# Attention with a fused maxout layer: a fifth group transposed by DMA, loads placed behind the crossbar transposes, the last tile stored by halves

## The chip, the cores and the metric

The kernel runs on one core of a Trainium2 chip. The metric is device time in microseconds, from the start of the program to its end. TensorE (PE) does the matmuls, VectorE (DVE) and ScalarE (ACT) work on elements, GpSimd (POOL) copies and issues loads, SyncE (SP) issues transposes and stores. Each engine runs its own list of instructions in order and waits at semaphores for the others. POOL, SP and ACT each have a queue of their own for the DMAs that they issue; the 16 DMA engines of the core are common to all.

## What is computed

Attention over 8 batches, 12 heads, 448 positions and 64 dimensions, with one added to the softmax's denominator, and behind it a layer that takes the larger of three projections:

```python
scores = scale * np.matmul(q, k.transpose(0, 1, 3, 2))
m = np.max(scores, axis=-1, keepdims=True)
e = np.exp(scores - m)
attn = e / (np.sum(e, axis=-1, keepdims=True) + np.exp(-m) + 1e-09)
x = np.matmul(attn, v)          # then (B*S, H*D) = (3584, 768)
h = np.maximum(np.maximum(x @ w1, x @ w2), x @ w3)   # each 768 x 768
out = h @ w_out
```

All inputs and the output are float32 in memory; the loads convert to float16.

## The kernel before

**Groups.** Heads are taken four at a time (GH = 4): 3 groups to a batch, 24 groups in all, numbered i. A batch is complete for the projections when its three groups are.

**What a group needs.** load_qk(i) issues the loads of k and q, load_v(i) those of v in two parts, all from POOL (lines 103, 113, 116). The q and k of a group must be transposed to have the head dimension on the partitions. For the first groups (i < PE_QK) transpose_pe does this in two halves of 11 PE transposes each (line 181), and an engine given as an argument evicts the results from PSUM (evac, lines 168 and 170). For the others transpose_dma issues two crossbar DMA transposes from SP, of q and then of k (line 211), and shift_q afterwards moves blocks of the result between the partition halves with four copies (line 219). prep_v (lines 357 to 360) copies v into the layout that the matmuls read: on DVE for the first groups, on POOL for i >= PE_QK.

**Buffers.** Loaded tiles have four buffers of each kind, KT and QT (the transposed k and q) three, the prepared v three. The transpose of group i+2 can therefore start only when the scores of group i-1 are done. The PSUM pool ps_s has three buffers, shared by score tiles, attention results and PE transposes of the later first groups.

**The order of work.** It is written out by hand. After a prologue, batch 0's three groups are done by halves (parts "E" and "O"), which gives the up-projections something to start on. Then the main loop runs over i = 3 to 23. Each iteration has three visits (vi = 0, 1, 2): scores of group i for two, two and three units (scores, line 274, and their exps on ACT, line 294); in the first two visits the attention of group i-1 (av_tail, line 314, reading vt, then av_main, line 331, and the normalization on DVE); then filler. x_transpose_dma(i-1) puts the attention's result into xT with one crossbar transpose from SP (line 384).

**Filler.** A list of pieces: up_piece (line 401: six or more matmuls, result taken over by DVE at 410 or 412) and out_piece (line 424: a tile of 128 rows by 384 columns; DVE scales it into o_sb at 431). add_batch(b) appends a batch's pieces at the visits given in the dictionary adds, fill(cols) takes as many as the given number of columns pays for, and share(n) spreads what is left evenly up to the next addition. Whatever is left after the loop runs at the end, then all of the last batch.

**Stores.** When both column halves of an output tile are in o_sb, two stores of 64 rows each go out on SP (line 443), one behind the other.

**POOL's list in the main loop** is, for each iteration: the loads of v for group i+2 and of k, q for group i+3; prep_v(i), if i >= 6; shift_q(i+2), which waits for the crossbar transpose. SP's is: two transposes of group i+2, the x transpose of group i-1, and stores as they fall due.

Of the kernel before, what the change touches and what calls it, by code (L numbers as in the profile page):

```python
# [12 lines left out]
AF = mybir.ActivationFunctionType  # L13
ALU = mybir.AluOpType
ts = bass.ts

MMDT = FP16
LAMBDA = 256.0
# [3 lines left out]
def kernel(  # L22
# [29 lines left out]
    scale = 1.0 / math.sqrt(D)  # L52


    PE_QK = 6
    NEB = 2
    NV = 3

# [49 lines left out]
    def load_v(i):  # L108
        b, g = groups[i]
        t = ld_pool.tile([P, GH, 5, D], MMDT, tag="ld_v", name="ld_v")  # L110
        raw.setdefault(i, {})["v"] = t
        src = v[b].rearrange("(g h) (p t) d -> g p h (t d)", g=NG, t=T)[g]
        nc.gpsimd.dma_start(  # L113
            out=t[0:HP, :, 1:5].rearrange("p h t d -> p h (t d)"), in_=src[:, :, 0 : 4 * D]
        )
        nc.gpsimd.dma_start(  # L116
            out=t[HP:P, :, 0:4].rearrange("p h t d -> p h (t d)"), in_=src[:, :, 3 * D : T * D]
        )
# [53 lines left out]
    def transpose_pe(i, pr, pool, k_eng, q_engs):  # L172

        if pool is ps_s:
            both = ps_s.tile([128, 2, 1024], MMDT, tag="s", name="trT")
            tps = [both[:, 0], both[:, 1]]
        else:
            tps = [ps_b.tile([128, 1024], MMDT, tag="b", name="trT") for _ in range(2)]
        kr, qr = raw[i]["k"], raw[i]["q"]
        def tr(n, j, src, t):  # L180
            nc.tensor.transpose(  # L181
                out=tps[n][:, ts(j, 128)],
                in_=src[:, t + 1 : t + 3, :].rearrange("x t d -> x (t d)"),
                identity=ident16,
            )

        kj = (0, 1, 2) if pr == 0 else (3, 4, 5, 6)
        qt = (-1, 1, 3, 5, 0, 2, 4, 6) if pr == 0 else (8, 10, 12, 7, 9, 11, 13)
        for j, b in enumerate(kj):
            tr(0, j, kr, 2 * b)  # L190
        for j, t in enumerate(qt):
            tr(1, j, qr, t)
        if i not in KT:
            KT[i] = att_pool.tile([P, T * 128], MMDT, tag="KT", name="KT")
            QT[i] = att_pool.tile([P, (NB + 1) * 128], MMDT, tag="QT", name="QT")
        evac(
            k_eng,
            KT[i][:, kj[0] * 128 : (kj[-1] + 1) * 128],
            tps[0][:, 0 : len(kj) * 128],
        )  # L200
        q0 = pr * 1024
        n = -(-len(qt) // len(q_engs))
        for e, eng in enumerate(q_engs):
            a, b = e * n * 128, min((e + 1) * n, len(qt)) * 128
            evac(eng, QT[i][:, q0 + a : q0 + b], tps[1][:, a:b])
# [10 lines left out]
    def shift_q(i, eng):  # L216
        t = QT[i]
        for d0, s0, o, a, n in ((0, HP, 1, 4, 3), (HP, 0, 0, 4, 4), (0, HP, 11, 7, 4), (HP, 0, 11, 8, 3)):
            eng.tensor_copy(  # L219
                out=t[d0 : d0 + HP, o * 128 : (o + n) * 128],  # L220
                in_=t[s0 : s0 + HP, a * 128 : (a + n) * 128],
            )
# [131 lines left out]
    def prep_v(i, eng):  # L354
        t = raw[i].pop("v")
        vx, vt = v_buf[i % NV], vt_buf[i % NV]
        eng.tensor_copy(out=vx[:, :, :, 0:D], in_=t[:, :, 1:4, :])  # L357
        t2 = t.rearrange("p (r h) t d -> p r h t d", r=NP)
        eng.tensor_copy(out=vt[0:HP, :, 0:D], in_=t2[0:HP, :, 0, 4, :])
        eng.tensor_copy(out=vt[HP:P, :, 0:D], in_=t2[HP:P, :, 1, 0, :])  # L360
# [53 lines left out]
    NH = 2  # L414
    NW = DM // NH
    order = (0, 2, 4, 6, 1, 3, 5)

    def out_piece(bp, t, nh):
        if nh == 0:
            outs[0] = out_pool.tile([128, DM], FP32, tag="o_sb", name="o_sb")  # L420
        o_sb = outs[0]
        op_ps = ps_b.tile([128, 512], FP32, tag="b", name="op_ps")
        for fc in range(NFC):
            nc.tensor.matmul(  # L424
                out=op_ps[:, 0:NW],
                lhsT=hT[bp][:, fc, ts(t, 128)],
                rhs=wout_sb[:, fc, ts(nh, NW)],
                start=(fc == 0),
                stop=(fc == NFC - 1),
            )  # L430
        nc.vector.tensor_scalar(  # L431
            out=o_sb[:, ts(nh, NW)],
            in0=op_ps[:, 0:NW],
            scalar1=1.0 / LAMBDA,
            scalar2=None,
            op0=ALU.mult,
        )
        if nh == NH - 1:
            for half in range(2):
                n = 2 * t + half  # L440
                b = 2 * bp + n // T
                rows = out[b * S : (b + 1) * S].rearrange("(p t) m -> t p m", t=T)
                nc.sync.dma_start(out=rows[order[n % T]], in_=o_sb[half * HP : half * HP + HP])


    UP = NDC * (S + 6)
# [20 lines left out]
    def fill(cols):  # L467
        credit[0] += cols
        while pieces and credit[0] > 0:
            f, a, w = pieces.pop(0)  # L470
            f(*a)
            credit[0] -= w
        if not pieces:
            credit[0] = min(credit[0], 0.0)
# [24 lines left out]
    for n, (part, g) in enumerate(parts):  # L499
        ej = n % NEB  # L500
        pp, pg = parts[n - 1] if n > 0 else (None, None)
        step = UPE if n > 2 else 0
        nxt = g + 1 if part == "E" and g < NG - 1 else None
        scores(g, ej, (0, 1), part)
        if n != 3:
            scores(g, ej, (2, 3), part)
        if n > 0:
            av(pg, 1 - ej, 0, pp)
        if n > 1 and n != 4:
            x_transpose_pe(parts[n - 2][1], parts[n - 2][0])  # L510
        if n == 3:
            av(pg, 1 - ej, 1, pp)
            scores(g, ej, (2, 3), part)
        fill(step)
        if nxt is not None and n > 0:
            transpose_pe(nxt, 0, ps_b, AC, (DV,))
        fill(step)
        scores(g, ej, (4, 5), part)
        scores(g, ej, (6,), part)
        if n == 0:  # L520
            warm(4)
            transpose_pe(nxt, 0, ps_b, DV, (DV,))
        if n == 3:
            x_transpose_pe(pg, pp)
            add_up(0, 0, NE, [(i, f) for i in range(3) for f in (0, 2, 4)])
        if nxt is not None:
            transpose_pe(nxt, 1, ps_b, DV, (DV,))
        if n > 0 and n != 3:
            av(pg, 1 - ej, 1, pp)
        fill(step)  # L530
        if n == 5:
            transpose_pe(3, 1, ps_s, DV, (DV,))
        fill(step)
        if n == 0:
            prep_v(0, DV)
        if n == 1:
            load_weight(2)
        if n == 2:
            load_v(3)
            load_qk(4)  # L540
            load_weight(3)
        if n == 4:
            load_v(4)
            load_qk(5)
            transpose_pe(3, 0, ps_s, DV, (DV,))


    visits = ((0, 1), (2, 3), (4, 5, 6))
    adds = {3 * (3 * b + 4) + 1: b for b in range(1, B - 1)}

    def share(n):

# [3 lines left out]
    for i in range(3, NI):  # L556
        ej, pj = (i + 1) % NEB, i % NEB
        first = i == 3
        if i + 2 < NI and i + 2 >= PE_QK:
            transpose_dma(i + 2)  # L560
        if first:
            load_v(5)
            load_qk(6)
        elif i + 2 < NI:
            load_v(i + 2)
            if i + 3 < NI:
                load_qk(i + 3)
        for vi, units in enumerate(visits):
            n = 3 * i + vi
            scores(i, ej, units)  # L570
            if vi < 2:
                av(i - 1, pj, vi, "O" if first else "EO")
            if vi == 1:
                prep_v(i, nc.vector if i < PE_QK else nc.gpsimd)
                if not first:
                    x_transpose_dma(i - 1)
            if n in adds:
                add_batch(adds[n])
            per = UPE if first and vi < 2 else share(n)
            if vi == 0 and first:  # L580
                x_transpose_pe(1, "O")
            if vi == 2 and first:
                fill(per / 2)
                x_transpose_pe(i - 1, "O")
                add_up(0, NE, NO, [(w, f) for w in range(3) for f in (0, 2, 4)])
                add_out(0)
                per = share(n)
            if vi > 0 and i + 1 < PE_QK:
                fill(per / 2)
                transpose_pe(i + 1, vi - 1, ps_s, DV, (DV,))  # L590
                fill(per / 2)
            else:
                fill(per)
        if i + 2 < NI and i + 2 >= PE_QK:
            shift_q(i + 2, nc.gpsimd)

    av(NI - 1, NI % NEB, 0, "EO")
    av(NI - 1, NI % NEB, 1, "EO")
# [34 lines left out]
```

The softmax here doesn't subtract the row's maximum and nothing guards it: scores larger than these inputs give would overflow.

## Time and profile before

| | |
|---|---|
| median of 8 runs | 343.94 us (343.52 to 344.77) |
| the profiled execution, its own time | 343.89 us |
| its span in the profile | 342.0 us |
| PE clock granted | 1.0 of full speed |
| HBM read, written | 44.04 MB, 11.01 MB |

The profile is of one execution. Its span runs from the first to the last instruction; the time of the execution is 1.9 us longer. Of what follows, a timeline line has start, length, engine, line, operation, output and inputs, how many instructions are merged in it and, in brackets, how long the engine had been idle and what ended that. A line of the table of waits has who waited for whom, total us, how often, and the longest. The slices on the page are 40 equal parts of the span with the busy share in tenths.

The costliest groups (line, engine, operation, output and inputs, shape, count, busy us and mean ns of one, idle us before it and its releaser):

```profile
L294 ACT ACTIVATE e<-stp 128x896 f16<-128x896 f32 (+4 forms) x171 | 144.0, 903 | 145.0 <-PE stp L274 144.9
L401 PE MATMUL p_i<-xT,w 128*128 128x448 f16 (+2 forms) x972 | 173.6, 332 | 0.5 <-DVE o_sb L431 0.3
```

PE spends half its time in up_piece and hardly ever waits there; ACT idles as long as it works, waiting for scores.

### The profile page before, as it was taken

Reading aid. Unit: us, or ns where it says so; the run is one execution under the profiler, and the core shown is the slowest. Engines: PE = TensorE matmul, PEld = TensorE weight load, DVE = VectorE, ACT = ScalarE, POOL = GpSimd, SP = SyncE. Lnnn points to the kernel's source line nnn. Section 1 sums busy time; section 2 is a strip of 40 time slices with the busy share of each in tenths; the row PEclk is TensorE's granted clock in tenths of the full one; section 3 lists DMA queues with packets and bytes.
Section 4 is the critical chain, followed back from the end, with each engine's and each line's share of the span. In section 5 each row is a group of like instructions: output and inputs, shape, how many; then the busy total and the mean of one; then the engine's idle time right before and its main releaser. Section 6 shows DMA issues by size and latency. Waiting matters only on the chain.

```text
span 342.0 us, 9746 instructions
## 1 busy us (share of the span) xinstructions
PE 328.9 (96%) x4157; PEld 197.9 (58%) x4157; DVE 189.3 (55%) x418; ACT 146.3 (43%) x174; POOL 139.4 (41%) x247
## 2 busy tenths in 40 slices
PE   7889988999999999999999999999999999999994
PEld 3568767855555655555555555555556655465552
DVE  2565666755556456456556556555556555565552
ACT  2873366575544453543544453543544443300000
POOL 8773542637659066173377076074445000000000
PEclk9999999999999999999999999999999999999999
DMA  7999999999999999989988999979960460133006
GB/s 112 197 207 209 205 200 151 151 137 229 208 170 116 167 218 134 126 119 222 123 137 118 180 206 128 136 111 217 155 114 3 124 125 4 31 76 95 2 18 167
DMA packets 89499, 47.42 MB, mean 139 GB/s; under 512 B 58224, under 2 KB 85872, under 8 KB 89456
## 3 DMA queue, kind: packets, MB, share of 16 engines
q0 software_dynamic: 29392, 22.03, 46.3%
q1 hardware_dynamic: 60064, 24.78, 41.4%
q8 instruction: 32, 0.52, 0.6%
q14 instruction: 11, 0.09, 0.1%
HBM read 44.04 MB, written 11.01 MB: 161 GB/s over the span
## 4 chain that ended last, share of the span: by engine, by line
PE 89%; DMA 3%; DVE 3%; ACT 2%; issue 1%; POOL 0%; SPq 0%; ACTq 0%; DVEq 0%; POOLq 0%
PE p_i L401 48%; PE op_ps L424 15%; PE avp L331 11%; PE stp L274 11%; DMA out_dram<-o_sb 2%; PE avp L314 2%; ACT e L294 2%; PE trT L181 2%; DMA ld_k<-in_k_dram 1%; DVE QT L170 1%; DVE o_sb L431 0%; DVE xn L347 0%; DVE xT L380 0%; PE xtp L374 0%; PE warm L155 0%
## 5 line engine op out<-in xcount | busy, mean ns | idle before, releaser
L294 ACT ACTIVATE e<-stp 128x896 f16<-128x896 f32 (+4 forms) x171 | 144.0, 903 | 145.0 <-PE stp L274 144.9
L401 PE MATMUL p_i<-xT,w 128*128 128x448 f16 (+2 forms) x972 | 173.6, 332 | 0.5 <-DVE o_sb L431 0.3
L401 PEld LDWEIGHTS <-w 128*128 128x128 f16 x972 | 89.8, 98 | 68.4 <-issue 5.7
L412 DVE TENSOR_TENSOR hT<-hT,p_i 128x448 f16<-128x448 f16 (+2 forms) x96 | 59.6, 621 | 43.3 <-PE p_i L401 43.1
L219 POOL COPY QT<-QT 64x384 f16<-64x384 f16 (+1 forms) x72 | 40.1, 556 | 101.9 <-DMA QT<-ld_q 85.3
L424 PE MATMUL op_ps<-w,hT 128*128 128x384 f16 x336 | 58.3, 327 | 0.0
L274 PE MATMUL stp<-QT,KT 64*64 64x448 f16 (+2 forms) x756 | 47.9, 339 | 3.2 <-ACT e L294 1.9
L431 DVE TENSOR_SCALAR o_sb<-op_ps 128x384 f32<-128x384 f32 x56 | 31.0, 556 | 26.2 <-PE op_ps L424 23.3
L331 PE MATMUL avp<-vx,e 128*128 128x65 f16 x1152 | 45.4, 194 | 0.0
L424 PEld LDWEIGHTS <-hT 128*128 128x128 f16 x336 | 31.6, 98 | 23.2 <-issue 2.1
L410 DVE CAST hT<-p_i 128x448 f16<-128x448 f32 (+2 forms) x48 | 29.9, 624 | 23.7 <-PE p_i L401 23.6
L331 PEld LDWEIGHTS <-e 128*128 128x128 f16 x1152 | 38.8, 97 | 2.2
L347 DVE TENSOR_TENSOR xn<-avp,rb 128x512 f16<-128x512 f32 (+1 forms) x54 | 34.1, 632 | 1.9
L274 PEld LDWEIGHTS <-KT 64*64 64x64 f16 x756 | 15.8, 105 | 28.0 <-issue 24.3
L341 DVE TENSOR_SCALAR rb<-avp 128x8 f32<-128x8 f32 (+1 forms) x54 | 8.9, 165 | 40.0 <-PE avp L331 40.0
L314 PEld LDWEIGHTS <-e 64*64 64x64 f16 x768 | 14.4, 107 | 9.2 <-DVE QT L170 0.8
L103 POOL DMA_DIRECT2D ld_q<-in_q_dram x24 | 17.7, 737 | 4.3 <-PE avp L331 1.7
L103 POOL DMA_DIRECT2D ld_k<-in_k_dram x25 | 17.9, 716 | 3.1 <-DMA w<-in_moe_w_out_dram 1.5
L357 POOL COPY vx<-ld_v 128x768 f16<-128x768 f16 x20 | 16.4, 819 | 5.4 <-issue 2.9
L314 PE MATMUL avp<-vt,e 64*64 64x65 f16 x768 | 15.6, 193 | 1.3 <-DVE QT L170 0.6
L116 POOL DMA_DIRECT2D ld_v<-in_v_dram x24 | 15.2, 633 | 2.6 <-DMA w<-in_moe_w_out_dram 1.2
L113 POOL DMA_DIRECT2D ld_v<-in_v_dram x24 | 15.2, 635 | 2.4 <-DVE rb L341 1.5
(33 smaller groups left out, 83.6 us busy)
## 6 DMA issues: line engine op xcount, KB each, us to landing
out_dram<-o_sb SPq DMA_DIRECT2D x56, 192.0 KB, 3.1
ld_v<-in_v_dram POOLq DMA_DIRECT2D x48, 128.0 KB, 4.8
ld_q<-in_q_dram POOLq DMA_DIRECT2D x24, 224.0 KB, 7.2
ld_k<-in_k_dram POOLq DMA_DIRECT2D x23, 224.0 KB, 6.7
w<-in_moe_w_dram POOLq DMA_DIRECT2D x9, 384.0 KB, 9.7
w<-in_moe_w_out_dram POOLq DMA_DIRECT2D x3, 384.0 KB, 10.9
xT<-xn SPq DMA_TRANSPOSE x21, 4.4
QT<-ld_q SPq DMA_TRANSPOSE x18, 6.0
```

Source lines behind the costliest of these rows:

```text
L103: nc.gpsimd.dma_start(out=tiles[nm][:, 1 : NP * T + 1].rearrange("x (r t) d -> x r (t d)", r=NP)[:, p0:p1], in_=src[:, p0:p1],)
L219: eng.tensor_copy(out=t[d0 : d0 + HP, o * 128 : (o + n) * 128], in_=t[s0 : s0 + HP, a * 128 : (a + n) * 128],)
L274: nc.tensor.matmul(out=stp[half * HP : half * HP + HP, par, j * qn : (j + 1) * qn], lhsT=k_block(i, pr, h2, x[half]), rhs=q_cols(i, pr, h2 ...
L294: nc.scalar.activation(out=dst, in_=src, func=AF.Exp, scale=scale)
L314: nc.tensor.matmul(out=ps[half * HP : half * HP + HP, hh, j * D1 : (j + 1) * D1], lhsT=eF[hh * HP : hh * HP + HP, o : o + HP], rhs=vt[hh * ...
L331: nc.tensor.matmul(out=ps[:, hh, j * D1 : (j + 1) * D1], lhsT=eF[:, o : o + 128], rhs=vx[:, 2 * pr + hh, (x[0]), 0:D1], start=False, stop= ...
L347: nc.vector.tensor_tensor(out=xn[i][:, pr, ws[0] : ws[0] + nw].rearrange("p j h d -> p h j d"), in0=acc[:, :, :, 0:D], in1=rb[:, :, 0:nw]. ...
L401: nc.tensor.matmul(out=p_i[:, j * qn : (j + 1) * qn], lhsT=w_sb[i][:, dc, ts(fc, 128)], rhs=xT[b][:, dc, q0 : q0 + qn], start=(dc == 0), s ...
L410: nc.vector.tensor_copy(out=dst, in_=src)
L412: nc.vector.tensor_tensor(out=dst, in0=dst, in1=src, op=ALU.max)
L424: nc.tensor.matmul(out=op_ps[:, 0:NW], lhsT=hT[bp][:, fc, ts(t, 128)], rhs=wout_sb[:, fc, ts(nh, NW)], start=(fc == 0), stop=(fc == NFC - 1),)
L431: nc.vector.tensor_scalar(out=o_sb[:, ts(nh, NW)], in0=op_ps[:, 0:NW], scalar1=1.0 / LAMBDA, scalar2=None, op0=ALU.mult,)
```

## The change

1. PE_QK goes from 6 to 5: group 5 is transposed by DMA, shifted on POOL, and its v prepared on POOL.
2. In the main loop the PE transposes of group 4 (the only ones left there) stand in visits 0 and 1, ahead of the filler, and are evicted by ACT; before, they stood in visits 1 and 2 in the middle of the filler and DVE evicted them.
3. From iteration 4 on, the loads are called at the end of the iteration, behind shift_q, for groups one further on; iteration 4 has both calls.
4. A batch's pieces are added one visit later.
5. In the prologue prep_v(0) moves ahead of a transpose, and one eviction is split between ACT and DVE.
6. The last output tile is stored as four pieces, by row half and column half, the row halves on SP and ACT; its last column half is scaled half by DVE and half by ACT.

```diff
-    PE_QK = 6
+    PE_QK = 5
...
+    def store(o_sb, bp, t, half, cols, eng):
+        n = 2 * t + half
+        b = 2 * bp + n // T
+        rows = out[b * S : (b + 1) * S].rearrange("(p t) m -> t p m", t=T)[order[n % T]]
+        eng.dma_start(out=rows[:, cols], in_=o_sb[half * HP : half * HP + HP, cols])
+
     def out_piece(bp, t, nh):
+        last = bp == B // 2 - 1 and t == 6
...
-        nc.vector.tensor_scalar(
-            out=o_sb[:, ts(nh, NW)],
...
+        if last and nh == NH - 1:
+            hw = NW // 2
+            c = nh * NW
+            nc.vector.tensor_scalar(
+                out=o_sb[:, c : c + hw], in0=op_ps[:, 0:hw], scalar1=1.0 / LAMBDA, scalar2=None,
+                op0=ALU.mult,
+            )
+            nc.scalar.activation(
+                out=o_sb[:, c + hw : c + NW], in_=op_ps[:, hw:NW], func=AF.Copy, scale=1.0 / LAMBDA
+            )
+        else:
+            nc.vector.tensor_scalar(
+                out=o_sb[:, ts(nh, NW)],
...
+        if last:
+            store(o_sb, bp, t, 0, ts(nh, NW), nc.sync)
+            store(o_sb, bp, t, 1, ts(nh, NW), nc.scalar)
+        elif nh == NH - 1:
+            store(o_sb, bp, t, 0, slice(0, DM), nc.sync)
+            store(o_sb, bp, t, 1, slice(0, DM), nc.sync)
...
         if n == 0:
             warm(4)
             transpose_pe(nxt, 0, ps_b, DV, (DV,))
+            prep_v(0, DV)
...
         if nxt is not None:
-            transpose_pe(nxt, 1, ps_b, DV, (DV,))
+            transpose_pe(nxt, 1, ps_b, DV, (AC, DV) if n == 0 else (DV,))
...
-        if n == 0:
-            prep_v(0, DV)
...
-    adds = {3 * (3 * b + 4) + 1: b for b in range(1, B - 1)}
+    adds = {3 * (3 * b + 4) + 2: b for b in range(1, B - 1)}
...
-        if first:
-            load_v(5)
-            load_qk(6)
-        elif i + 2 < NI:
-            load_v(i + 2)
-            if i + 3 < NI:
-                load_qk(i + 3)
+        def loads(iv, iq):
+            if iv < NI:
+                load_v(iv)
+            if iq < NI:
+                load_qk(iq)
+
+        if i < 5:
+            loads(i + 2, i + 3)
...
-            if vi > 0 and i + 1 < PE_QK:
-                fill(per / 2)
-                transpose_pe(i + 1, vi - 1, ps_s, DV, (DV,))
-                fill(per / 2)
-            else:
-                fill(per)
+            if vi < 2 and i + 1 < PE_QK:
+                transpose_pe(i + 1, vi, ps_s, AC, (AC,))
+            fill(per)
         if i + 2 < NI and i + 2 >= PE_QK:
             shift_q(i + 2, nc.gpsimd)
+        if i >= 4:
+            loads(i + 3, i + 4)
```

More of the change, by code (lines that the diff above doesn't have):

```diff
@@ L430, in out_piece @@
             )
-        nc.vector.tensor_scalar(
-            out=o_sb[:, ts(nh, NW)],
[L433 to L443, printed above, removed]
+        if last and nh == NH - 1:
[11 more added lines that the diff above has]
+                out=o_sb[:, ts(nh, NW)],
+                in0=op_ps[:, 0:NW],
+                scalar1=1.0 / LAMBDA,
+                scalar2=None,
+                op0=ALU.mult,
+            )
+        if last:
[4 more added lines that the diff above has]
+            store(o_sb, bp, t, 1, slice(0, DM), nc.sync)
     UP = NDC * (S + 6)
```

## The prediction

> **What bounds the kernel now.** I read the page first, then the table of waits, then the timeline of POOL and of all engines around 56 to 92 us, and last the DMA view of short windows.
>
> The page's busy shares, the PE and DMA slices:
>
> ```profile
> PE 328.9 (96%) x4157; PEld 197.9 (58%) x4157; DVE 189.3 (55%) x418; ACT 146.3 (43%) x174; POOL 139.4 (41%) x247
> ...
> PE   7889988999999999999999999999999999999994
> ...
> DMA  7999999999999999989988999979960460133006
> ```
>
> PE is busy for 328.9 of 342.0 us. Of the 13.1 us left, 5.3 lie before 40 us, 2.3 between 40 and 60, 0.3 at 120 and 5.1 behind the last matmul. So what PE no longer does comes off the end, and what makes PE wait goes onto it. The second line to see is DMA: full until some 150 us. A transfer added early finds no free room.
>
> The table of waits:
>
> ```profile
> POOL QT L219 <- DMA QT<-ld_q: 85.3, 14, 11.1
> ...
> PE stp L274 <- ACT e L294: 1.9, 3, 0.9
> ```
>
> POOL spends 85 us at the head of shift_q (L219), waiting for a crossbar transpose, and everything behind it on POOL waits too: the next loads, and prep_v. PE's score matmuls wait for ACT three times only (0.16 us early, 0.89 in each of groups 3 and 4), and PE never waits for POOL. How near POOL comes to that is in POOL's timeline (start, length, line):
>
> ```profile
> 57.18 2.38 POOL L219 COPY QT<-QT 64x384 f16<-64x384 f16 x4 [6.99 <-DMA QT<-ld_q]
> 59.51 0.62 POOL L113 DMA_DIRECT2D ld_v<-in_v_dram  x1
> ...
> 61.42 0.73 POOL L103 DMA_DIRECT2D ld_q<-in_q_dram  x1
> 64.90 2.43 POOL L219 COPY QT<-QT 64x384 f16<-64x384 f16 x4 [2.75 <-DMA QT<-ld_q]
> ...
> 71.10 0.29 POOL L360 COPY vt<-ld_v 64x128 f16<-64x128 f16 x1
> 78.53 2.38 POOL L219 COPY QT<-QT 64x384 f16<-64x384 f16 x4 [7.14 <-PE avp L331]
> ...
> 84.67 0.29 POOL L360 COPY vt<-ld_v 64x128 f16<-64x128 f16 x1
> ```
>
> and in the timeline of all engines:
>
> ```profile
> 71.90 1.22 SPq L211 DMA_TRANSPOSE QT<-ld_q  x1
> ...
> 75.89 2.30 SPq L384 DMA_TRANSPOSE xT<-xn  x1
> ...
> 77.38 0.30 PE L314 MATMUL avp<-vt,e 64*64 64x65 f16 x16
> ...
> 80.83 3.56 PE L401 MATMUL p_i<-xT,w 128*128 128x448 f16 x18
> ...
> 87.79 0.30 PE L314 MATMUL avp<-vt,e 64*64 64x65 f16 x16
> ```
>
> The shifts at 57.18, 64.90 and 78.53 are those of groups 6, 7 and 8. The prep_v copies that end at 71.4 and 85.0 are groups 6 and 7; the attention that reads them starts on PE at 77.38 and 87.79: 6.0 and 2.8 us to spare. The up-projection of batch 1 begins at 80.83, just as the crossbar transpose of 75.89 lands (5.1 us after issue). Prep 7 trails the QT transpose of group 8 (71.90) by 13.1 us: landing 6.5, shift 2.4, four load issues 2.7, three copies 1.5. That transpose waits for its q load, issued at 61.42, landed 10.4 us later. So groups 5 to 8, where the filler between attention visits is thin, are where a late load reaches PE.
>
> **Part by part.**
>
> *Group 5 by DMA.* PE loses 22 transposes, two batches of 11 at 0.61 us in the chain:
>
> ```profile
> 59.97 0.61 PE trT L181 x11
> ```
>
> that is -1.22, all on the path. The wait for ACT that those transposes' PSUM buffers caused in iteration 4 (0.89 us before the matmuls at 58.49) goes too: -0.89. DVE loses four evictions and prep 5 and isn't on the path. SP gains two transposes (issue 1.3 and 1.4 us) ahead of those of group 6; POOL gains one shift (2.4 us) and prep 5 (1.45 us).
>
> *Batch additions one visit later.* Work is only moved, but the light visits get lighter. By the order of the built program, iterations 4 and 5 end with 12 score matmuls and only 12 filler matmuls (0.69 + 1.10 us) before the next scores. Three exps take 2.54 us and start 0.49 after the scores, so they end at 3.03; PE wants the third score buffer at about 2.3 to 2.55. I put down 0.7 for each of the two: +1.4 (0 if the buffers come free sooner, 2 at most).
>
> *Evictions of group 4 on ACT, first in the visit.* Iteration 3 gets 3.0 us of ACT copies (0.49 + 1.02 + 0.60 + 0.92, from the copies of 384 and 512 columns at 0.49 and 0.60, 0.84 ns a column) beside 7 exps (5.95). ACT, 9.0 us, is then as long as PE there (9.82 less 1.23 waits). I reckon 1.4 us of waits in place of 1.23: +0.15 (0 to +1).
>
> *First groups.* prep_v(0) goes ahead on DVE (0.7 us) and half an eviction goes to ACT, whose first exp of group 1 starts some 0.25 us later; the attention no longer waits 0.26 for vt. +0.1 (-0.2 to +0.3).
>
> *Last tile.* Before, the last eviction (336.88, 0.56 us) is followed by two store issues on SP, 0.47 and 0.58, and each lands 2.6 after its issue. After, the halves are issued side by side on SP and ACT: the second issue, 0.5 to 0.6, drops out. The half eviction would be 0.35 in place of 0.56 on DVE, but ACT first issues its earlier store (about 0.5, from 336.48) and copies after that, up to 337.4, so nothing is gained there. -0.6 (-0.9 to -0.3).
>
> Sum without new waits on POOL: -1.22 - 0.89 + 1.4 + 0.15 + 0.1 - 0.6 = -1.1, a span of 340.9.
>
> *Loads.* On POOL the order "shift, loads of the next two groups, prep" is the same in both programs from group 7 on: the later place in the source brings nothing there. What changes is the front. Before, the loads of v6, k7, q7 go out at 46.5 to 50.2 behind nothing. Now they stand behind shift 5. That shift waits for transpose 5, which waits for q5 (issued 38.71, landed 10.2 later, 48.96), lands 4.2 later like group 6's (52.81), 53.3, and ends at 55.7. Then the loads of set 6 go out from 55.6 to 58.3, shift 6 (its data there since about 57.4) to 60.7, the loads of set 7 to 63.4 and prep 5 to 64.9, which is early enough (attention 5 at about 68).
>
> What it costs is DMA time. A set is 0.72 MB, 3.6 us at the 201 GB/s that the loads reach alone (42 to 52 us). Set 6 used to be through by 56; now most of it comes behind transpose 6 and the x transpose of group 3, which occupies the queues up to 61:
>
> ```profile
> GB/s 266 266 276 276 246 89 10 0 0 0 0 0 0 0 0 0 0 0 0 3 7 7 10 10 7 10 10 7 14 7 48 256 297 280 297 297 247 263 270 249
> ```
>
> This is 58 to 61 us of before in 40 slices. The v load issued at 59.51 doesn't move while the transpose is in its silent stretch. I take 1 us of set 6 as done before that and 2.6 us as left at 61. Before, the trio that follows (transposes 7, set 7, x transpose 4: 2.75 + 3.6 + 3.0 = 9.35 us by their shares and bytes) took 11 us, 61 to 72. With 2.6 us more at the same ratio it takes 3.1 longer: transpose 8 is issued at 75.0 and not 71.90, and prep 7 is done 13.1 later, at 88.1.
>
> When does PE want it? Iteration starts after, by the order of PE's instructions and the lengths before (9.82, 10.05, 7.80, 7.67, 10.41 for 3 to 7): 51.4, 58.9, 67.5, 75.1, and 84.2 for iteration 8, since three light visits now stand in 7. Attention 7 is due at 84.7. **Wait: 3.4 us.** On the way prep 6 (shift 7 at 69.8, done 76.3, due 75.6) takes 0.7 of it and the x transpose of group 5 (issued 77.6 behind transpose 8, landed 82.7, wanted at 81.4 plus 0.7) a little more; the three aren't added, since each delay puts the next due time off. Behind it prep 8, 94.5 against 101, has room again. The bounds: 0.3 if transpose 8 stays at 71.90 (prep 7 at 85.0 against 84.7), 6.9 if it slips to 78.5.
>
> The Trainium skill (DMA: Bandwidth & Descriptors, "Queues, rings and completion order") speaks for a smaller price: each DMA engine takes packets from its queue rows in turn, so loads would fill a silent transpose. By that set 6 would cost nothing more and the wait would be 0.3. The row above, with a load issued and nothing moving for more than a microsecond, says otherwise, and I go by the row.
>
> Sum: 340.9 + 3.4 = 344.3, against 342.0: +2.3. The profiled execution took 343.89, 1.9 over its span, the median is 343.94; so 346.2.
>
> **Rivals.**
>
> *The slack holds (faster).* The missing set 6 finds the two silent stretches (59.2 to 60.7 and 70.0 to 71.4), and with no loads queued transposes 5 and 6 land in the 2.9 us that is the least on record. Transpose 8 then stays by 72 and the wait by 0.3 to 0.5: span 341.0 to 341.4, time 342.9 to 343.2, less if the 1.4 us of ACT waits don't come (341.5). It decides at transpose 8: up to 72.2. For it: those stretches, and that DMA isn't full after 56. Against it: the load that stood still at 59.51.
>
> *It cancels (no change).* Transpose 8 between 72.2 and 73.6, wait 0.5 to 1.9: 343.3 to 344.6. The moved loads, which keep their old order from group 7 on, then do nothing, and the transposes saved pay for one shift.
>
> *Later still.* Transpose 5 holds up q6, with which it shares the queues (both through only at 55.5); transpose 6, shift 5, set 6 and all behind slip by 2 us and more: transpose 8 at 78.5, wait 6.9, 349.7. It decides at q6: landed after 55. For it: KT of group 7 shared with loads and landed 11.3 us after issue. Against: q7 landed in 6.6 beside transpose 6.
>
> **How the numbers follow.** Forecast 0.43 (own range 344.7 to 348), faster rival 0.24, no change 0.18, later still 0.15. Differences under 0.2% (343.25 to 344.63) can't be told from none. Slower 0.58, same 0.18, faster 0.24. The range runs from 342.0 to 349.0, leaving out a part of each outer rival.
>
> **What would show it.** In the profile after: 22 fewer transposes at L181 and PE busy about 1.2 us less; ACT evictions at 42 to 48; shift 5 ending near 55.7 with load issues right behind; the q transpose of group 8 issued near 75; PE idle, 2 to 4 us in all, before the L314 matmuls or the first p_i between 74 and 90, released by POOL vt or by xT; POOL's prep 7 ending near 88; ACT waits of 0.7 at about 58 and 66; the last store issued near 337.4 once on each queue. I am wrong if PE has no idle between 70 and 90, or if waits of this kind come back in later groups.

## The result, and the profile after

| | before | after |
|---|---|---|
| median | 344.01 us (343.43 to 345.54, 32 runs) | 348.30 us (345.26 to 349.20, 11 runs) |
| ratio, 95% interval | | 1.0102 [1.0084, 1.0119] |
| the profiled execution, its span | 343.89, 342.0 us | 347.07, 345.3 us |

The change makes the kernel 1% slower. The eleven times of after stand in three groups by their mean granted TensorE clock: 345.3 and 345.4 at 1.0, 346.8 to 347.1 at 0.995, and 348.3 to 349.2 at 0.987 or 0.988. The profiled one is of the middle group. A ratio leaves out executions that are more than 1.5% above the fastest of their kernel and lies near the quotient of the mean times, so it can differ from the quotient of the medians given beside it, which rest on all executions.

The page after, busy shares and the two slice lines that answer to those of before:

```profile
PE 329.9 (96%) x4135; PEld 197.7 (57%) x4135; DVE 184.9 (54%) x406; ACT 149.5 (43%) x180; POOL 143.0 (41%) x254
...
PEclk9999999998999999999999999999999999999999
DMA  7999999999999999999989999997991250124006
```

PE has 22 matmuls fewer and yet 1.0 us more busy time: a clock below full stretches busy time too, and one slice of PEclk, the tenth (78 to 86 us), shows an 8. The table of waits of PE (who waited for whom, total us, times, longest):

```profile
PE avp L314 <- POOL vt L359: 2.9, 1, 2.9
...
PE stp L274 <- ACT QT L168: 0.9, 1, 0.9
PE avp L314 <- ACT e L294: 0.9, 2, 0.4
```

The first line is new: PE never waited for POOL before. The second is the wait of 0.89 that iteration 3 had before too, then put down to an exp. The third is a part of the price of the lighter visits. Where the first is, PE's timeline shows (start, length, engine, line, operation, and in brackets the idle time before and what ended it):

```profile
75.28 0.57 PE L274 MATMUL stp<-QT,KT 64*64 64x448 f16 x8
78.80 0.78 PE L314 MATMUL avp<-vt,e 64*64 64x65 f16 x16 [2.94 <-POOL vt L359]
79.51 1.50 PE L331 MATMUL avp<-vx,e 128*128 128x65 f16 x24
80.82 1.99 PE L431 MATMUL op_ps<-w,hT 128*128 128x384 f16 x6
82.74 0.57 PE L274 MATMUL stp<-QT,KT 64*64 64x448 f16 x8
83.14 0.30 PE L314 MATMUL avp<-vt,e 64*64 64x65 f16 x16
83.37 0.93 PE L331 MATMUL avp<-vx,e 128*128 128x65 f16 x24
84.13 1.14 PE L431 MATMUL op_ps<-w,hT 128*128 128x384 f16 x6
```

Iteration 7 begins at 75.28; the attention of group 6 stands still until prep_v(6) has written vt. The next two lines are the same work as the last two, at about half the pace: 1.50 against 0.93, 1.99 against 1.14. From the start of the attention to the next scores it is 3.94 us in the first visit (78.80 to 82.74) and 2.06 in the second (83.14 to 85.20). So the late vt costs twice: PE, due at 75.68 (0.40 after the scores, as in the second visit), starts 3.1 late, and then takes 1.9 longer for the same work, 1.7 of it by the granted clock (0.50 over the 3.42 us from 79.14 to 82.56). POOL over the same time:

```profile
55.60 2.40 POOL L219 COPY QT<-QT 64x384 f16<-64x384 f16 x4 [8.75 <-DVE rb L341]
57.95 0.63 POOL L113 DMA_DIRECT2D ld_v<-in_v_dram  x1
...
72.65 2.38 POOL L219 COPY QT<-QT 64x384 f16<-64x384 f16 x4 [5.57 <-PE op_ps L431]
74.98 0.64 POOL L113 DMA_DIRECT2D ld_v<-in_v_dram  x1
75.60 0.64 POOL L116 DMA_DIRECT2D ld_v<-in_v_dram  x1
76.21 0.74 POOL L103 DMA_DIRECT2D ld_k<-in_k_dram  x1
76.91 0.74 POOL L103 DMA_DIRECT2D ld_q<-in_q_dram  x1
77.70 0.82 POOL L357 COPY vx<-ld_v 128x768 f16<-128x768 f16 x1
78.46 0.29 POOL L359 COPY vt<-ld_v 64x128 f16<-64x128 f16 x1
```

Shift 5 ends at 57.95 and set 6 (v6, k7, q7) goes out behind it. Transpose 7 needs q7. On SP it was issued at 58.92 before,

```profile
58.92 1.69 SPq L211 DMA_TRANSPOSE QT<-ld_q  x1
```

and after at 65.30, as the load of q7, issued at 59.88 (before: 49.49), had landed 5.3 us later:

```profile
65.30 1.25 SPq L211 DMA_TRANSPOSE QT<-ld_q  x1
...
72.33 1.22 SPq L211 DMA_TRANSPOSE QT<-ld_q  x1
```

Shift 7 begins at 72.65; the releaser named, PE, is not the real one: transpose 7 landed 7.2 us after its issue, at 72.5. Behind the shift come four load issues (set 8), and only then prep 6.

### The profile page after: what moved, and what is told of

Read it like the earlier page. It is cut to its first block, busy times and chain, and to the rows that moved or that the text cites. A ratio compares the mean times of both kernels' runs of the same rounds, so it can differ in the third digit from the quotient of the medians.

```text
span 345.3 us, 9716 instructions
## 1 busy us (share of the span) xinstructions
PE 329.9 (96%) x4135; PEld 197.7 (57%) x4135; DVE 184.9 (54%) x406; ACT 149.5 (43%) x180; POOL 143.0 (41%) x254
## 2 busy tenths in 40 slices
DMA packets 91515, 47.88 MB, mean 139 GB/s; under 512 B 60112, under 2 KB 88016, under 8 KB 91472
## 4 chain that ended last, share of the span: by engine, by line
PE 88%; ACT 4%; POOL 2%; issue 2%; DVE 2%; DMA 1%; ACTq 0%; POOLq 0%
PE p_i L401 47%; PE op_ps L431 15%; PE avp L331 11%; PE stp L274 10%; ACT e L294 3%; PE avp L314 2%; PE trT L181 1%; DMA ld_k<-in_k_dram 1%; POOL QT L219 1%; POOL ld_q L103 0%; ACT QT L168 0%; DVE QT L170 0%; DVE xT L380 0%; PE warm L155 0%; PE xtp L374 0%
## 5 line engine op out<-in xcount | busy, mean ns | idle before, releaser
L219 POOL COPY QT<-QT 64x384 f16<-64x384 f16 (+1 forms) x76 | 42.3, 556 | 100.8 <-DMA QT<-ld_q 76.4
L431 PE MATMUL op_ps<-w,hT 128*128 128x384 f16 x336 | 59.1, 330 | 0.0
L357 POOL COPY vx<-ld_v 128x768 f16<-128x768 f16 x21 | 17.2, 819 | 4.1 <-DMA ld_v<-in_v_dram 1.6
L113 POOL DMA_DIRECT2D ld_v<-in_v_dram x24 | 15.3, 636 | 2.8 <-DVE xT L380 1.5
```

What stands on the lines that cost most here:

```text
L219: eng.tensor_copy(out=t[d0 : d0 + HP, o * 128 : (o + n) * 128], in_=t[s0 : s0 + HP, a * 128 : (a + n) * 128],)
L431: nc.tensor.matmul(out=op_ps[:, 0:NW], lhsT=hT[bp][:, fc, ts(t, 128)], rhs=wout_sb[:, fc, ts(nh, NW)], start=(fc == 0), stop=(fc == NFC - 1),)
```

## Experiments

Each ratio is to the kernel before, run on the same chip beside it (its medians: 343.72 to 344.09), with its 95% interval. Diffs are against the kernel named in the heading.

### Before, with group 5 by DMA and nothing else

```diff
-    PE_QK = 6
+    PE_QK = 5
```

> The kernel before with PE_QK = 5 and nothing else of the change: the loads keep their old places in the source, but set 6 still stands behind shift 5 on POOL. Theory (group 5 by DMA puts every load from set 6 on behind one more transpose and shift on POOL): prep 6 ends near 79, attention 6 is due near 75.4, so PE waits 3 to 3.5 us for vt there, and then runs some 3 us at half clock; -1.2 -0.9 +3.4 +1.5 on the span of before: 344.5 to 345.5, time 346.0 to 347.5. Rival (the wait comes of the loads' new place, of the batch additions or of the moved transposes): no wait for vt, time 341.5 to 342.5.

Measured: 349.54 us, 1.0154 [1.0119, 1.0188]. One line of the change is slower by 1.5%, more than the whole change. Its waits of PE:

```profile
PE avp L314 <- POOL vt L359: 3.2, 1, 3.2
PE p_i L401 <- DMA xT<-xn: 1.7, 1, 1.7
```

The wait for vt is the one expected (prep 6 at 79.2, half clock behind it). The second, for the x transpose of group 5, was not: its 1.7 us are most of the 2 us by which the forecast was too low. The rival falls: neither the loads' new place nor the other parts are needed to make the wait.

### Before, with two transposes that nobody uses

```diff
+        if first:
+            spare = [att_pool.tile([P, T * 128], MMDT, tag="sp_" + nm, name="sp_" + nm, bufs=1) for nm in "qk"]
+            for dst, nm in zip(spare, "qk"):
+                nc.sync.dma_start_transpose(
+                    out=dst.rearrange("p (j x) -> p j x", x=P),
+                    in_=raw[5][nm][:, 1 : NB + 1].rearrange("x t d -> x (t d)"),
+                )
```

> The kernel before, group 5 still transposed by PE, with two more crossbar transposes on SP at the start of iteration 3, of the same q and k of group 5 into tiles that nobody reads. No shift and no load stands behind them on POOL: they only take room in the DMA queues and on SP, ahead of transpose 6. Order theory (what costs is that set 6 stands behind shift 5 on POOL): set 6 goes out as before, prep 6 and 7 keep 2.8 us and more, at most 1 us of waits: 343.5 to 345. Volume theory (the queues are full until 150 us, so a transpose more makes what follows late, whatever the order): waits for vt or xT of 2 us or more between 74 and 103, half clock behind them: 346 to 349.5.

Measured: 345.82 us, 1.0070 [1.0044, 1.0096], between the two forecasts. PE's waits and SP's timeline, of an execution of 347.10:

```profile
PE p_i L401 <- DMA xT<-xn: 3.1, 1, 3.1
```

```profile
49.06 1.32 SPq L562 DMA_TRANSPOSE sp_q<-ld_q  x1
50.43 3.34 SPq L562 DMA_TRANSPOSE sp_k<-ld_k  x1
53.90 4.63 SPq L211 DMA_TRANSPOSE QT<-ld_q  x1
58.62 1.44 SPq L211 DMA_TRANSPOSE KT<-ld_k  x1
...
76.76 1.73 SPq L211 DMA_TRANSPOSE QT<-ld_q  x1
```

Transpose 6 is issued over 4.6 us, shift 6 begins at 62.9 where it was 57.2, and transpose 8 goes out at 76.8 (before: 71.9). Nothing on POOL was put behind the spare pair. So two transposes more delay the supply by 5 us and bring a wait of 3 us, here without half clock behind it; prep 6 (74.4) and 7 (87.5) come 3.0 and 2.5 us later than before and are still ahead of PE. The run doesn't part room in the DMA queues from time on SP, where the spare pair and transpose 6 of q take 9.3 us to issue. Of the two halves of the mechanism, this room is one, the order behind shift 5 the other (the next run); the volume theory is half right, the order theory's "at most 1 us" is refuted. The runs don't split the 5.6 us of the run before exactly, since the waits displace each other. The volume is small: 47.88 MB against 47.42, all of it in a stretch where the queues are full.

### After, with set 6 ahead of shift 5

```diff
-    ld_pool = ctx.enter_context(tc.tile_pool(name="ld", bufs=4))
+    ld_pool = ctx.enter_context(tc.tile_pool(name="ld", bufs=5))
...
-        if i < 5:
-            loads(i + 2, i + 3)
+        if first:
+            loads(5, 6)
+            loads(6, 7)
```

> The changed kernel, group 5 still by DMA, but the loads of v6, k7, q7 stand on POOL ahead of shift 5, and the load tiles have five buffers in place of four, because with four k7 waits for transpose 5 of k. Theory (order on POOL): set 6 is loaded at 47 to 51, transpose 7 starts at 58 to 60 and not 65.3, prep 6 is done by 72 to 74, no wait at attention 6, span 340.7 to 342.2 (shift 5 may now be late by up to 1.5 us for the scores of group 5, since transpose 5 shares the queues with set 6). Rival (DMA work as such: one more pair of transposes early on is what costs): prep 6 still ends after 77 and PE waits 2 us or more near 75: 345 to 348.

Measured: 346.83 us, 1.0088 [1.0056, 1.0119]: the rival's time, but prep 6 ends at 75.2. Attention 6 has no wait any more; instead PE stands still before the scores of group 5:

```profile
57.52 1.08 PE L401 MATMUL p_i<-xT,w 128*128 128x192 f16 x11
60.09 0.24 PE L401 MATMUL p_i<-xT,w 128*128 128x192 f16 x1 [1.49 <-issue]
60.63 1.01 PE L274 MATMUL stp<-QT,KT 64*64 64x448 f16 x8 [0.30 <-DMA KT<-ld_k]
61.24 0.62 PE L314 MATMUL avp<-vt,e 64*64 64x65 f16 x16
61.80 1.50 PE L331 MATMUL avp<-vx,e 128*128 128x65 f16 x24
```

Transpose 5, now beside set 6's loads, lands 10.5 us after its issue in place of 5.8, so shift 5 begins at 59.8 and not 55.6. The lengths of the last two lines show the half clock again, here behind 1.49 and 0.30 us of idling. Putting the order right moves the shortage, it doesn't end it.

### After, with prep 6 on DVE; then x transposes first on SP; then additions at visit 1

```diff
-                prep_v(i, nc.vector if i < PE_QK else nc.gpsimd)
+                prep_v(i, nc.vector if i < 7 else nc.gpsimd)
```

> The changed kernel with prep_v of groups 5 and 6 on DVE in place of POOL. Theory (POOL's list): the 3.1 us that PE idles at 75.7 to 78.8 are prep 6, which stands on POOL behind shift 7 and the loads of set 8; DVE can do it at once, v6 has long landed. PE then waits for nothing there, the clock stays at 1.0, and the span falls by 3.1 for the wait and 1.5 for the half clock behind it: 340.7, time 342.5, and runs no longer spread over 4 us. Shift 7 ends at 75.0, 0.2 before its scores, so up to 0.5 may remain. Rival (DMA): the transposes are late whoever prepares v, the wait goes over to the scores of group 7 or to batch 1's xT, and the time stays above 346. Rival (thin visits): PE simply runs out of work early, the wait stays at the same place under another name, 346 to 348.

Measured: 344.83 us, 1.0037 [1.0008, 1.0066]. The 2.9 us for vt is gone, attention 6 starts at 76.15, and the clock stays at 1.0. Two thirds of the loss come back (1.0102 to 1.0037); a part of the rest has a new place (this profile is of 344.47 us; the times still spread from 342.9 to 348.5, and what the long ones wait for isn't shown):

```profile
PE p_i L401 <- DMA xT<-xn: 1.8, 1, 1.8
```

So POOL's prep was what PE waited for there, as the theory has it, and the next late transfer stands right behind, as the rival has it. The second run took that on, in addition to the first edit:

```diff
-        if i + 2 < NI and i + 2 >= PE_QK:
+        if i < 6 and i + 2 >= PE_QK:
             transpose_dma(i + 2)
...
                     x_transpose_dma(i - 1)
+                if i >= 6 and i + 2 < NI:
+                    transpose_dma(i + 2)
```

> The run with prep 6 on DVE, and SP issues the x transpose of group i-1 ahead of the transposes of group i+2 from iteration 6 on. Theory (the 1.8 us for xT in that run is only its place behind transpose 8 on SP): x transpose 5 is issued near 73.4 and has landed by 81, no wait for xT, no half clock: 342.6 to 343.3. Rival (the DMA queues are full there, so it lands no sooner, or transpose 8 is late for its group): a wait of 1 us or more for xT, QT or vt between 80 and 103, 344.2 to 345.5.

Measured: 352.38 us, 1.0203 [1.0153, 1.0253], the slowest of all. The wait for xT is gone and another is there (this profile is of its shortest execution, 348.22 us):

```profile
98.63 0.57 PE L274 MATMUL stp<-QT,KT 64*64 64x448 f16 x8
101.54 0.78 PE L314 MATMUL avp<-vt,e 64*64 64x65 f16 x16 [2.33 <-POOL vt L359]
102.25 1.50 PE L331 MATMUL avp<-vx,e 128*128 128x65 f16 x24
```

Now it is prep 8: transpose 9, issued at 87.07, landed 8.2 us later (shift 9 begins at 95.36), and prep 8 stands behind that shift and four load issues. Kind and place are the rival's (vt, between 80 and 103), the price is far above its 345.5. Four of the six times are 352 and more, at a granted clock of 0.988 to 0.990, and no profile is of these, so their 4 us more aren't shown. The third run adds the pieces at visit 1 as well (the one-line edit is shown further down):

> The same, with a batch's pieces added at visit 1 again, as before. Theory (the later additions cost 1.5 to 1.8 us in waits for ACT at the ends of iterations 4 and 5): those waits are gone, and x transpose 5, due some 2.5 us sooner, is still in time: 341.0 to 342.0. Rivals: the waits for ACT come of the ACT evictions and not of the additions, then no change against the run without this edit; or xT is waited for again, 1 to 2 us: 342.3 to 343.5.

Measured: 347.39 us, 1.0047 [1.0016, 1.0078], its times spread from 344.3 to 355.0. No forecast held. The profiled execution is among the longest (352.38) and waits for vt (2.1), KT (1.2) and others (3.3); one such profile doesn't say which of these is typical, so the run shows no more than its time.

### After, with PE kept busy in the wait

```diff
+            if n == 21:
+                warm(12)
             if vi < 2:
                 av(i - 1, pj, vi, "O" if first else "EO")
```

> The changed kernel with 12 matmuls of 512 columns on a constant tile, 2.6 us, put before the attention of group 6, into the stretch in which PE idles; the output is not touched. Theory (the idle stretch throttles the clock, which costs 1.5 us in the profiled run and more in the slower ones): PE is busy through the wait, attention 6 still starts at 78.8 to 79, the granted clock stays at 1.0, span 343.6 to 343.9, time 345.3 to 345.7, with the spread of the runs down from 4 us to under 1. Rival (the clock has another cause): half clock at 79.4 to 82.8 as before, no gain, 346 to 349.

Measured: 345.36 us, 1.0051 [1.0035, 1.0068]; times 344.96 to 346.76, a spread of 1.8 us where after has 3.9. Twelve matmuls on zeros stand where PE had idled (75.75 to 78.51), attention 6 begins at 78.55, and PE then runs at full speed. The windows (us, busy time and count of each engine, granted clock, DMA share, GB/s) of after and of this run:

```profile
79.00:80.00 1.00, 0.87 (x25) 0.78 (x24) 0.00 (x0) 0.00 (x0) 0.88 (x3) 0.57 1.68 152
80.00:81.00 1.00, 1.00 (x20) 0.96 (x18) 0.00 (x0) 0.00 (x0) 0.94 (x2) 0.50 1.14 161
81.00:82.00 1.00, 1.00 (x5) 0.46 (x3) 0.88 (x3) 0.00 (x0) 0.96 (x2) 0.50 1.31 203
82.00:83.00 1.00, 1.00 (x11) 0.35 (x13) 0.33 (x2) 0.00 (x0) 1.00 (x3) 0.72 1.28 236
```

```profile
80.00:81.00 1.00, 1.00 (x13) 0.42 (x10) 0.83 (x3) 0.00 (x0) 0.90 (x3) 1.00 1.29 168
```

The wait stays, the clock loss goes. It was worth 2.9 us of after's median (348.30 to 345.36), or 1.7 by the two ratios (1.0102 and 1.0051), since the median of after lies in the upper of its three groups. One stretch of 3.42 us at half clock costs 1.7 us, and the three groups of after lie about that far apart; that they have none, one and two such stretches isn't shown, as only the middle one has a profile.

### After, with additions at visit 1

```diff
-    adds = {3 * (3 * b + 4) + 2: b for b in range(1, B - 1)}
+    adds = {3 * (3 * b + 4) + 1: b for b in range(1, B - 1)}
```

> The changed kernel with a batch's pieces added at visit 1, as before. The prediction's view (the later additions only cost: 1.8 us of waits for ACT at the ends of iterations 4 and 5): those waits go, attention 6 still waits for vt until about 79, and some 1.2 us more of PE's work is done by then: time 345.5 to 347. Rival (group 5 alone, with additions at visit 1, also waited 1.7 us for xT of group 5: the later additions put that due time off by one visit): the waits for ACT go, a wait of 1 to 2 us for xT comes near 85: 348 to 350.

Measured: 349.12 us, 1.0151 [1.0132, 1.0171]. The rival's time, but not its mechanism:

```profile
75.25 0.75 PE L274 MATMUL stp<-QT,KT 64*64 64x448 f16 x8
80.36 0.78 PE L314 MATMUL avp<-vt,e 64*64 64x65 f16 x16 [4.36 <-POOL vt L359]
```

The waits for ACT at the ends of iterations 4 and 5 go, as the prediction's view has it. Iteration 7 begins at 75.25 as in after, prep 6 is 1.5 us later (transpose 7, issued at 65.41, landed after 8.8 us), and no xT is waited for. In the profiled execution (349.03 us) the longer idle stretch is followed by 6.8 us at half clock (79.9 to 86.7) in place of 3.4. The other three took as long (348.83 to 349.45) at a mean clock of 0.994 or 0.995, which is that of the middle group of after, so the longer half clock isn't the general reason. Both views priced this part wrong: with group 5 by DMA, the later additions save 1.7 us (0.5% of 344) and don't cost any.

### The parts that need no DMA

With PE_QK = 6 in the changed kernel:

> The changed kernel with group 5 transposed by PE again (PE_QK = 6), all else as changed, so its transposes are evicted by ACT like group 4's. Theory (POOL's list): no shift 5 and no prep 5 on POOL, set 6 is loaded at 46 to 50 as before the change, prep 6 is done near 71 and attention 6 due near 77: no wait, clock 1.0. What is left is -0.43 in the prologue, -0.53 at the end, +0.3 twice for ACT's evictions in iterations 3 and 4, +0.9 to 1.8 for the exps that hold the score buffers: span 342.5 to 343.5, time 344.3 to 345.3. Rival (thin visits and ACT are the loss): 346 or more, with PE idle near 75 still. Rival (the load calls moved to the end of the iteration are the loss): the same, with the loads of sets 7 and 8 later than before the change.

Measured: 344.57 us, 1.0022 [1.0002, 1.0041]; no wait for vt (prep 6 ends at 70.0), the waits for ACT as in after (0.7 and 0.9 us, before the attention at 61.22 and 69.86). The theory's time holds, both rivals fall. Prologue and last tile alone on the kernel before:

> The kernel before with parts 5 and 6 of the change alone (prologue, last tile); main loop as before. Theory: both gains read in the trace of after are real and add up, -0.4 and -0.5: 342.7 to 343.1. Rival: the prologue's gain is only given back at the next wait for a DMA or for ACT: 343.1 to 343.4; or neither shows: 343.5 to 344.

Measured: 343.63 us, 0.9985 [0.9965, 1.0004]: can't be told from none by itself. The theory's 342.7 to 343.1 doesn't hold. In the profile the tail, from the last eviction to the end, is 4.74 us where it was 5.12. The prologue's gain isn't there: iteration 3 begins at 41.75 (before: 41.64); over the eleven profiles with the new prologue it begins between 41.18 and 41.78, 41.5 in the mean, over the three with the old one between 41.64 and 41.95, 41.8 in the mean. Next, the same with the PE transposes first in visits 0 and 1, evicted by DVE, then by ACT:

```diff
-            if vi > 0 and i + 1 < PE_QK:
-                fill(per / 2)
-                transpose_pe(i + 1, vi - 1, ps_s, DV, (DV,))
-                fill(per / 2)
-            else:
-                fill(per)
+            if vi < 2 and i + 1 < PE_QK:
+                transpose_pe(i + 1, vi, ps_s, DV, (DV,))
+            fill(per)
```

> The run with prologue and last tile alone, and the PE transposes of groups 4 and 5 first in visits 0 and 1, as in the change, but evicted by DVE as before. Theory (the two waits of 0.89 for ACT in groups 3 and 4 come of the transposes that take a score buffer in visit 2): they go, -1.2 to -1.8 against the run without this edit: 341.8 to 342.6. Rivals: the x transpose of group 5, which lands just as it is wanted, is then waited for: 342.8 to 343.6; or the wait for ACT only moves to visits 0 and 1: 343.3 to 343.8.

Measured: 344.03 us, 1.0017 [0.9997, 1.0037]: no gain, and above the theory's range. Group 3 keeps its wait of 0.89; that of group 4 has changed its releaser and grown:

```profile
59.73 0.38 PE L274 MATMUL stp<-QT,KT 64*64 64x448 f16 x4 [1.45 <-DVE QT L170]
```

```diff
-                transpose_pe(i + 1, vi, ps_s, DV, (DV,))
+                transpose_pe(i + 1, vi, ps_s, AC, (AC,))
```

> The kernel before with prologue, last tile and part 2 alone: the PE transposes of groups 4 and 5 first in visits 0 and 1 and evicted by ACT; group 5 by PE, loads and additions as before. Theory (with additions at visit 1 the visits are heavy enough, so the wait of 0.89 in group 4 goes, and ACT's extra copies cost nothing): 0.9 less than with prologue and last tile alone (343.6 median): 342.6 to 343.2, faster than before by 0.2% or more. Rivals: the wait only moves (to an eviction, as with DVE, or to x transpose 5, which lands just as it is wanted): 343.3 to 344.2; or ACT, now with 3 us of copies an iteration, makes scores wait in groups 3 and 4 by 1 us more: 344.5.

Measured: 342.83 us, 0.9966 [0.9952, 0.9980]: faster than before by 0.3%, and than after by 1.3% (0.9966 over 1.0102). This is the change without group 5 by DMA, without the later additions and without the moved loads. Iteration 4's wait for ACT falls from 0.89 to 0.2:

```profile
48.99 0.38 PE L274 MATMUL stp<-QT,KT 64*64 64x448 f16 x4 [0.89 <-ACT QT L168]
...
58.34 0.96 PE L274 MATMUL stp<-QT,KT 64*64 64x448 f16 x12
```

The twelve matmuls take 0.96 where undisturbed ones take 0.76. Group 3 keeps its 0.89. Iteration 3 takes 10.11 us, 0.28 more than with prologue and last tile alone, but no more than with DVE's evictions in the run above: what costs there is the place of the transposes, not ACT's copies. Against prologue and last tile alone the two intervals overlap, so part 2 by itself isn't clear of noise; against the same with DVE's evictions they don't. Beside the run with PE_QK = 6 this run also suggests what the later additions cost where PE hardly waits for transfers: 0.56% by the two ratios, 1.9 us, though the loads' places differ too; the two waits for ACT in that run's trace make 1.6 of it.

## Why the prediction was right, and where not

Slower was right (346.2 forecast, 348.30 measured), and so was the mechanism in the main: set 6 behind shift 5 on POOL and in full queues, then late transposes, then PE waiting for POOL's prep. Its steps:

- **Sum without new waits, -1.1.** The matmuls are 22 fewer, and the wait of 0.89 in iteration 4 is gone, as put down. The waits at the ends of iterations 4 and 5 are 0.88 each (59.36 where 58.48 was due, and 68.00), 1.8 against 1.4. Iteration 3 takes 10.11 against 9.82: +0.29 against +0.15, and by the runs with group 5 on PE not for ACT's copies but for the transposes' place. The tail gives -0.53 against -0.6. The prologue, put down at +0.1, gave -0.4 in this profile and about -0.3 in the mean of the profiles.
- **Loads.** Shift 5 ended at 57.95, not 55.7: transpose 5 landed 5.8 us after issue, not 4.2. Shift 7 began at 72.65, not 69.8: transpose 7 landed after 7.2, not 5.8. This is the term that was mis-sized. While transpose 7 was under way the loads moved 0.62 MB, where it was 0.30 in before, though the step itself said that set 6 would now share the queues. For transpose 5 this is no reason: 0.40 MB beside it, 0.36 beside the one it was priced by; why it took 1.6 us longer stays open.
- **Where PE waits.** The prediction put 3.4 us at prep 7 and had prep 6 take 0.7 of it (done 76.3, due 75.6). Prep 6 was done at 78.8 and took 3.1 of PE's time; prep 7 (85.6) was then far ahead of its due time at 89.8. The slip of transpose 8 to 75.0 on which the 3.4 rested didn't happen: it was issued at 72.33 (71.90 before). So the size was right and the place one group too late: the step from set 6 to transpose 8 failed, and that the wait came out near 3.4 is luck.
- **The clock** was left out altogether: 1.7 us by the granted clock in the profiled execution, 1.7 to 2.9 by the run that keeps PE busy. Without its loss the change takes 345.3 to 345.4 (the two executions at full clock, and the run that keeps PE busy), so the terms that the prediction did count came to 0.8 less than its 346.2. That 346.2 is no further from the median is luck too: waits priced too dear, and a cost that isn't in the sum.
- **Later additions, +1.4.** Read by itself the price is right (1.8 us in the trace of after, 1.9 between the two runs with group 5 on PE). With group 5 by DMA the part pays for itself by 1.7 us; in the profiles with and without it PE idles 2.94 and 4.36 us for vt, and the rest of the reason stays open.

Sum as measured, against the start of the last eviction (336.88 before, 340.71 after): -1.22 - 0.89 + 1.76 + 0.29 - 0.42 + 3.1 + 1.9 (the longer first visit) = 4.5, less 0.3 for a wait at 120 us that before had and after has not: 4.2, where 3.8 were measured. The last 0.4 isn't placed. With the tail of -0.53 the spans differ by 3.3.

Of the rivals, "the slack holds" failed at its own point of decision in another way than thought: transpose 8 was nearly in time (72.33), transpose 7 wasn't. By that sign "it cancels" (72.2 to 73.6) should have come true with a wait of 0.5 to 1.9; it was 3.1, so transpose 8 was the wrong sign to watch. "Later still" decided at q6, which was not what came late. The rule of the Trainium skill that was weighed (DMA: Bandwidth & Descriptors, "Queues, rings and completion order") would have made the wait 0.3; the runs with set 6 first and with the spare transposes show loads and transposes delaying each other by 4 to 5 us, so that price of nothing fails here. The row that was set against it shows less than was read from it: POOL's queue moves its first packet 1.6 us after the issue at 59.51, but 1.3 us after that of 248.75 too, where the DMA engines move nothing else. The load of 80.86 is the better witness: first packet after 2.8 us, behind a silent stretch (82.3 to 83.4 us, at most 15 GB/s).

## What to carry to other kernels

Work moved from the bounding engine to a queue that is full must be priced by what the queue then delivers late: the 1.2 us of transposes taken off PE cost 5.6 here (group 5 by DMA and nothing else). Where a wait comes of a shortage, an edit at the place of the wait hands it on (vt of group 6, xT of group 5, vt of group 8, KT of group 5); test with a run that adds or takes volume and leaves the order alone. Take a many-part change apart: the parts that needed nothing of the scarce queue were worth 0.3% by themselves.

## What the runs showed of the hardware

- An idle stretch of PE can cost as much again in clock, and not by its length alone. Idle 2.94 us: 3.4 us at half clock (after). Idle 2.33: half clock as well (x transposes first, 0.50 from 102 to 104). Idle 1.49 and, one matmul later, 0.30: half clock too (set 6 first, 0.50 from 62 to 64). Idle 4.36: 6.8 us at half clock. Idle 1.83 (prep 6 on DVE) and 3.09 (spare transposes, 82 to 85 us): none at all, the clock stays 1.00.
- The Trainium skill (TensorE: Matmul & The Clock Gate, "HAM oscillation — how this bites in real kernels") gives the rule that PE shouldn't idle for more than about 3.4 us. The half rate and its length of 3.4 agree with the windows of after; the threshold doesn't, as idle stretches of 1.5 (with the 0.3 behind it), 2.3 and 2.9 us were enough here.
- A crossbar transpose of q (loaded as 224 KB) landed 4.2, 5.8 and 6.5 us after issue in before (groups 6 to 8), and 5.8, 3.8, 7.2 and 4.0 in after (groups 5 to 8). That of group 5 took 10.5 us with set 6 loaded first: the loads moved 1.14 MB while it was under way, against 0.40 MB in after.
